# Rows of an expert's later places: gathered in quarter rows by 32 slots, and turned by VectorE in 32x32 squares instead of by TensorE

## The chip, the cores and the metric

The kernel runs on one core of one Trainium2 chip. The metric is the device time of one launch in microseconds (us), lower is better. Before the change three runs took 564.17, 568.13 and 568.21 us, median 568.13. The hardware profile was taken from one more execution, which took 564.15 us by its own clock and whose span, from the first to the last instruction, is 561.9 us.

## The reference, cut to what matters

Two steps, all in float32. A gated linear recurrence over 768 steps for 4 batches of 8 heads with 48 columns gives 3072 rows of 384 values. A mixture of experts without dropping then sends every row to one of 8 experts.

```
for t in range(S):                       # S = 768, per batch and head, state 48 x 48 complex
    S_re, S_im = a[t] * (S_re, S_im) + (k[t] outer v[t], 0)
    y[:, :, t] = q[t] @ S_re
x = y as (3072, 384)
expert = argmax(x @ w_gate); gate = softmax(x @ w_gate)[expert]
for e in range(8):                       # rows of expert e
    out[rows] = gate[rows] * (relu(x[rows] @ w1[e]) @ w2[e])     # w1[e] 384 x 1024, w2[e] 1024 x 384
```

## The kernel before

**Recurrence.** The first 272 us or so are the recurrence in chunks of 128 steps (6 chunks `u`, 4 batches `b`). TensorE does the chunk products, ScalarE and VectorE the gates, the rotations and the evictions. `finish` writes each finished 128 x 384 block of rows to a DRAM buffer `xd`. The order of this stage comes from a table `WHEN` of priorities, written out by hand: `put(t, f)` gives the instructions of `f` the priority `t`, and a scheduler lays each engine's queue out by it. `warm` issues matmuls that only keep TensorE running in the first microseconds.

**Routing.** `route` counts, for a group of chunks, which row goes to which expert, and adds it to `slots`, which holds for each expert and slot (slot = tile of 128 times lane) the row to read, the row to write and the gate. `first_place` names the busiest expert early; `places` orders the rest by their counts. An expert's position in that order is its place. Place `i` has room for `CAPS[i]` rows (448, 416, 416, 408, 400, 384, 376, 360), that is 4 tiles of 128 slots for places 0 to 4 and 3 tiles for 5 to 7; where a count is over its room, a slow path that is compiled in runs, which is not the case for these inputs. `gates_of_places` turns `slots` into `tok` (row to read), `row` (row to write) and `gate`, by place.

**Experts.** From about 272 us the 8 places are worked one after the other. Below, "place i" means the expert of place i, and (i, t) its tile t. Each has these steps:

- `load_w(i)`: SyncE loads w1 as `wa` (partition p, block k holds row 128k + p) and w2 as `wb`. Buffers alternate between two pools, so `wa` of place i + 2 waits until place i has done its first product, and `wb` until it has done its second.
- `gather(i)`: GpSimd (POOL) issues one indirect DMA for each tile of 128 slots: partition p gets the whole row of slot p (1536 bytes) of `xd`. The buffer `xg` alternates too, so the gather of place i + 2 waits until place i has been turned.
- `turn(i)`: the rows have to stand in columns for the product. TensorE transposes each 128 x 128 block with a matmul against `ident` into PSUM (`tp`, line 599), and ScalarE or VectorE copies it to `xt` (line 606). For the next place this is called inside `expert`, by `between`, two tiles before the end.
- `expert(i)`: the first product `hps` runs over 8 blocks `f` of 128 hidden units, all slots of the place at once; blocks alternate between ScalarE (odd f, line 633) and VectorE (even f, line 635) for the relu into `ht`. The second product `yps` runs tile by tile; VectorE multiplies it by the gate into `y` (line 647). A last tile of at most 64 rows is summed from parts: ScalarE copies to `z`, VectorE adds (lines 658 and 660) and multiplies (line 661).
- `scatter`: GpSimd writes the tile's rows to `out` by an indirect DMA (line 611).

The buffers that matter here: `psH` has 4 PSUM banks for `hps`, `psO` 2 for `yps`, `yp` has 3 buffers `y`. So a `y` waits until the scatter three tiles earlier has landed, and block f of `hps` waits until block f - 4 has been evicted. The scatters write one tensor, so each of them also waits until the one before it has landed. All gathers and scatters stand in one queue, POOL's, and run in its order.

`in_range(j)` reads the gates `a_re` and `a_im` once more in 6 parts (tiles `rc`, 768 KB each) and checks their range on VectorE, two passes for each part into `junk` (line 860). It only has to be done before the end.

Of the kernel before, what the change touches and what calls it, by code (L numbers as in the profile page):

```python
# [10 lines left out]
FP = mybir.dt.float32  # L11
I32 = mybir.dt.int32
# [10 lines left out]
LN_CAP = math.log(0.999)  # L23
A_MIN = 0.61
T_MAX = 1.5
CAPS = (448, 416, 416, 408, 400, 384, 376, 360)


# [8 lines left out]
def kernel(  # L37
# [28 lines left out]
    def mm(o, lhsT, rhs, start=True, stop=True):  # L66
        T["mm"] = nc.tensor.matmul(o, lhsT=lhsT, rhs=rhs, start=start, stop=stop, skip_group_check=True)  # L67
        return T["mm"]
# [9 lines left out]
    def const(shape, name, dt=FP):  # L78
        return cp.tile(shape, dt, name=name)
# [40 lines left out]
    for hp in range(HP):  # L120
        nc.gpsimd.tensor_copy(out=back[:, hp, 0:D], in_=ident[:, 0:D])
        nc.gpsimd.tensor_copy(out=back[:, hp, D:DD], in_=ident[:, 64 : 64 + D])

    M = const([P, NU, B, H], "M")
    acc = const([P, E], "acc")
# [263 lines left out]
    def small(shape, name, dt=FP):  # L389
        return ch.tile(shape, dt, tag=name, name=name, bufs=1)  # L390
# [64 lines left out]
    EARLY = 2  # L455
    owner = const([P, E], "owner", I32)
    own0 = const([P, 1], "own0", I32)
    tok = const([P, E, CT], "tok", I32)
    row = const([P, E, CT], "row", I32)
    gate = const([P, E, CT], "gate")  # L460
    over = const([P, 1], "over")
# [43 lines left out]
    def to_read(f, o):  # L505

        ts(out=o, in0=f, scalar1=-1.0, scalar2=0.0, op0=OP.add, op1=OP.max)
# [37 lines left out]
    def gates_of_places():  # L545
        f = small([P, E, CT], "fi")
        by_place(f, 2)
        to_read(f, tok)
        by_place(f, 0)
        to_write(f, row)  # L550
        by_place(gate, 1)
        cmp = small([P, E, E], "cmp")
        tt(out=cmp, in0=T["po"], in1=bc(T["cnt"], 1, E), op=OP.mult)
        o = small([P, E], "t8")
        nc.vector.reduce_sum(o, cmp, axis=AX_X)
        tt(out=o, in0=o, in1=caps, op=OP.is_gt)
        nc.vector.reduce_sum(over, o, axis=AX_X)


    def tiles(i):  # L560
        return -(-CAPS[i] // P)

    def load_w(i, after=None):
        o = own0 if i == 0 else owner[:, i : i + 1]
        ev = nc.sync.value_load(o[0:1, 0:1], min_val=0, max_val=E - 1)
        wa = EP[i % 2].tile([P, KD, F], FP, tag="wa", name="wa")
        ins = nc.sync.dma_start(out=wa, in_=w1[ds(ev, 1)].rearrange("o (i p) f -> p (o i) f", p=P))
        if after is not None:
            tc.add_manual_dep(ins.ins, after.ins.name, SYNC, reason="rows first")
        wb = EP[i % 2].tile([P, KF, DM], FP, tag="wb", name="wb")  # L570
        nc.sync.dma_start(out=wb, in_=w2[ds(ev, 1)].rearrange("o (i p) d -> p (o i) d", p=P))
        T["w", i] = wa, wb

    def gather(i, t0, t1, rows=N):

        if t0 == 0:
            T["xg", i] = EP[i % 2].tile([P, CT, DM], FP, tag="xg", name="xg")
        for t in range(t0, t1):
            n = min(P, CAPS[i] - t * P)
            nc.gpsimd.indirect_dma_start(  # L580
                out=T["xg", i][0:n, t],
                out_offset=None,
                in_=xd[0:rows, :],
                in_offset=bass.IndirectOffsetOnAxis(ap=tok[0:n, i, t : t + 1], axis=0),
                bounds_check=rows - 1,
                oob_is_err=False,
            )

    def turn(i, t0, t1, ps, end=None):

        xg = T["xg", i]
        if t0 == 0:
            T["xt", i] = EP[i % 2].tile([P, KD, CAPS[0]], FP, tag="xt", name="xt")
        c0, c1 = t0 * P, min(CAPS[i], t1 * P)
        for d in range(KD):
            tp = ps.tile([P, 512], FP, tag="tp", name="tp")
            for t in range(t0, t1):
                n = min(P, CAPS[i] - t * P)
                ins = nc.tensor.transpose(  # L599
                    out=tp[:, (t - t0) * P : (t - t0) * P + n],  # L600
                    in_=xg[0:n, t, d * P : (d + 1) * P],
                    identity=ident[0:n, 0:n],
                )
                if end is not None:
                    behind(ins, [end])
            T["turned"] = (nc.scalar.copy if d % 2 else nc.vector.tensor_copy)(
                out=T["xt", i][:, d, c0:c1], in_=tp[:, 0 : c1 - c0]
            )
# [11 lines left out]
    def expert(i, t0, t1, psH, psO, yp, between=None):  # L620

        xt = T["xt", i]
        wa, wb = T["w", i]
        if t0 == 0:
            T["ht", i] = EP[i % 2].tile([P, KF, CAPS[0]], FP, tag="ht", name="ht")
        ht = T["ht", i]
        c0, c1 = t0 * P, min(CAPS[i], t1 * P)
        for f in range(KF):
            ps = psH.tile([P, 512], FP, tag="tp" if psH is psT else "h", name="hps")[:, 0 : c1 - c0]
            for d in range(KD):  # L630
                mm(ps, wa[:, d, f * P : (f + 1) * P], xt[:, d, c0:c1], d == 0, d == KD - 1)
            if f % 2:
                nc.scalar.activation(out=ht[:, f, c0:c1], in_=ps, func=AF.Relu)  # L633
            else:
                ts(out=ht[:, f, c0:c1], in0=ps, scalar1=0.0, scalar2=None, op0=OP.max)  # L635
        for t in range(t0, t1):
            if t == t1 - 2 and between is not None:
                between()
            n = min(P, CAPS[i] - t * P)
            ps = psO.tile([P, DM], FP, tag="at" if psO is psA else "y", padded_shape=[P, 512], name="yps")  # L640
            g = gate[0:n, i, t : t + 1]
            y = yp.tile([P, DM], FP, tag="y", name="y")
            hs = ht[:, :, t * P : t * P + n]
            if n > 64:
                for f in range(KF):
                    mm(ps[0:n], hs[:, f], wb[:, f], f == 0, f == KF - 1)
                ts(out=y[0:n], in0=ps[0:n], scalar1=g, scalar2=None, op0=OP.mult)  # L647
            else:

                w = 32 if n <= 32 else 64  # L650
                parts = P // w
                for f in range(KF):
                    j = f % parts
                    mm(ps[j * w : j * w + n], hs[:, f], wb[:, f], f < parts, f >= KF - parts)
                z = yp.tile([P, DM], FP, tag="z", name="z")
                for j in range(1, parts):
                    nc.scalar.copy(out=z[j * w : j * w + n], in_=ps[j * w : j * w + n])
                tt(out=y[0:n], in0=ps[0:n], in1=z[w : w + n], op=OP.add)
                for j in range(2, parts):
                    tt(out=y[0:n], in0=y[0:n], in1=z[j * w : j * w + n], op=OP.add)  # L660
                ts(out=y[0:n], in0=y[0:n], scalar1=g, scalar2=None, op0=OP.mult)
            scatter(y, n, i, t)

    def early(t0, t1, end):

        turn(0, t0, t1, psT, end)
        expert(0, t0, t1, psT, psA, EP["y"])


    def put(t, f, *a):  # L670
# [5 lines left out]
        "l1": 0, "l2": 1, "p0": 2, "p1": 4, "p2": 4, "p3": 2, "p4": 4, "p5": 3, "s0.0.0": -8.68, "c0": True,  # L676
        "w0": -2.82, "s0.1.0": -7.5, "s0.2.0": -5.29, "s0.0.1": -10.26, "w1": -3, "s0.1.1": -8.3, "s0.2.1": -3.21,
        "s0.0.2": -9.64, "w2": -3, "s0.1.2": -6.91, "s0.0.3": -6.55, "w3": -3, "s0.1.3": -6.6, "h1": True,
        "s1.0.0": -2.81, "c1": False, "s1.1.0": -4.38, "s1.0.1": -4.06, "s1.1.1": -3.59, "d0.0": -3.83, "d0.1": -1.67,
        "TR0": -3, "a0.0": -3.0, "a0.1": -2.9, "a0.2": -2.8, "t0.0": -2.5, "r0.0": -0.4, "p.0": -1.18, "t0.1": -0.55,  # L680
        "r0.1": -1.5, "p.1": -0.32, "t0.2": -1.22, "r0.2": -1.0, "a1": -1.69, "LE1": -1.01, "s0.2.2": -0.84,
        "s0.2.3": -0.8, "d0.2": -0.76, "s1.0.2": -3.39, "s1.1.2": -3.19, "s1.0.3": -2.99, "s1.1.3": -2.79,
        "d1.0": -2.33, "d1.1": -1.18, "h2": False, "s2.0.0": -5.0, "c2": False, "s2.0.1": -6.16, "s2.0.2": -4.19,
        "s2.0.3": -6.99, "TR1": -1.69, "t1.0": -1.85, "r1.0": -1.59, "t1.1": -0.53, "r1.1": 0.42, "a2": -4.5,
        "results0": 1.02, "results1": 1.04, "state": 1.61, "evict": 1.11, "scores0": -0.86, "scores1": 0.42,
        "outer": 0.43, "finish": 1.53, "products": -1.42, "LE2": -6.28, "d2.0": -3, "d2.1": 0.0, "h3": False,
# [1 line left out]
        "r2.0": -3.02, "t2.1": -1.45, "r2.1": 0.68, "a3": -3.28, "LE3": -4.96, "d3.0": -2.87, "d3.1": -1.87,  # L688
        "h4": False, "s4.0.0": -7.27, "c4": False, "s4.0.1": -7.25, "g2": -3.01, "TR3": -2.37, "t3.0": -2.37,
        "r3.0": -1.87, "t3.1": -2.78, "r3.1": -0.87, "a4": -4.45, "LE4": -3.65, "s4.0.2": -7.47, "s4.0.3": -6.41,  # L690
        "d4.0": -2.59, "d4.1": -1.42, "h5": False, "s5.0.0": -6.32, "c5": False, "s5.0.1": -7.01, "s5.0.2": -6.82,
        "s5.0.3": -6.62, "TR4": -1.22, "t4.0": -2.13, "r4.0": -0.31, "t4.1": -0.56, "r4.1": 0.83, "a5": -6.92,
        "LE5": -5.71, "d5.0": -3.39, "d5.1": -1.51, "g4": -2.93, "TR5": -2.92, "t5.0": -2.34, "r5.0": -2,
        "t5.1": -2.31, "r5.1": -1,
    }

# [138 lines left out]
    T["second"]()  # L835
    gates_of_places()
    gather(0, EARLY, tiles(0))
    early(0, EARLY, end)
    att.close()

# [326 lines left out]
```

## Time and profile before

| what | value |
|---|---|
| median of 3 runs | 568.13 us (564.17 to 568.21) |
| profiled execution, own time | 564.15 us |
| its span | 561.9 us |
| TensorE busy, share of the span | 529.7 us, 94% |
| VectorE busy | 286.5 us, 51% |
| ScalarE busy | 217.8 us, 39% |
| GpSimd busy | 68.8 us, 12% (94 instructions) |
| mean granted TensorE clock | 0.99 |
| mean DMA rate | 131 GB/s over the span |

How to read it: TensorE has work in 94% of the span, and from 299 us to the end of the last product at 552 us it has no gap that the profile shows. A share of busy time is an average over the launch. [...] In the views below, PE is TensorE, PEld its weight loads, DVE VectorE, ACT ScalarE, POOL GpSimd and SP SyncE. L599 is line 599 of the kernel before.

### The profile page before, as it was taken

How to read it: one execution, taken by the hardware profiler on the slowest of the kernel's cores; microseconds unless marked ns; L12 is line 12 of the kernel's file. 1: busy time of each engine (PE TensorE's matmuls, PEld its weight loads, DVE VectorE, ACT ScalarE, POOL GpSimd, SP SyncE). 2: the span in 40 equal slices, each digit the busy share in tenths (PEclk: the TensorE clock that was granted, in tenths of full speed). 3: DMA queues.
4: the chain of work that ended last, by engine and by line, in shares of the span. 5: the costliest groups of instructions: out<-in, count | busy, mean ns of one | idle time of the engine just before them, and what ended most of it. 6: DMA issues, size and time to landing. Idle time of an engine off the chain costs nothing.

```text
span 561.9 us, 8229 instructions
## 1 busy us (share of the span) xinstructions
PE 529.7 (94%) x3221; PEld 376.7 (67%) x3221; DVE 286.5 (51%) x584; ACT 217.8 (39%) x330; POOL 68.8 (12%) x94
## 2 busy tenths in 40 slices
PE   3889979999999999999899999999999999999993
PEld 2666858877888888888768555555555555565651
DVE  5478687787889888784565174303113031211110
ACT  6867988786588764553201010101101011010100
POOL 2000000000000000001045301403031040101001
PEclk9979999999999999999999999999999999999998
DMA  9956691847646825404369975534234342230000
GB/s 166 205 80 102 112 148 35 160 76 151 117 86 123 160 58 118 72 30 173 139 255 313 387 281 223 179 127 147 59 144 144 127 153 89 83 121 25 15 14 29
DMA packets 166053, 73.39 MB, mean 131 GB/s; under 512 B 147725, under 2 KB 159031, under 8 KB 166008
## 3 DMA queue, kind: packets, MB, share of 16 engines
q1 hardware_dynamic: 162456, 63.12, 46.4%
q0 software_dynamic: 3552, 9.68, 5.0%
q8 instruction: 27, 0.44, 0.3%
q14 instruction: 18, 0.15, 0.1%
HBM read 63.26 MB, written 9.73 MB: 130 GB/s over the span
## 4 chain that ended last, share of the span: by engine, by line
PE 81%; DVE 6%; ACT 5%; DMA 4%; issue 2%; POOL 0%; ACTq 0%; DVEq 0%
PE yps L67 23%; PE hps L67 23%; PE tp L326 7%; PE at L67 6%; PE yt L67 6%; PE cst L67 4%; PE dk L67 3%; PE xb L67 3%; PE csl L67 2%; PE tp L599 2%; DMA xd<-x 2%; DMA xg<-xd,tok 1%; ACT R L169 1%; PE sp L67 1%; DVE ai L216 1%
## 5 line engine op out<-in xcount | busy, mean ns | idle before, releaser
L67 PE MATMUL yps<-wb,ht 128*128 128x384 f32 (+6 forms) x464 | 136.8, 489 | 0.0
L67 PE MATMUL hps<-xt,wa 128*128 128x416 f32 (+7 forms) x432 | 132.4, 465 | 0.0
L67 PEld LDWEIGHTS hps<-xt,wa 128*128 128x128 f32 x432 | 79.9, 190 | 50.1 <-issue 23.5
L67 PEld LDWEIGHTS yps<-wb,ht 128*128 128x128 f32 (+6 forms) x464 | 74.1, 175 | 52.9 <-issue 8.1
L633 ACT ACTIVATE ht<-hps 128x416 f32<-128x416 f32 (+7 forms) x36 | 16.8, 468 | 139.5 <-PE hps L67 128.3
L647 DVE TENSOR_SCALAR y<-yps,gate 128x384 f32<-128x384 f32 (+2 forms) x24 | 14.8, 617 | 102.6 <-PE yps L67 102.6
L67 PE MATMUL at<-qt,kt 96*128 96x128 f32 x384 | 54.2, 281 | 0.0
L611 POOL DMA_INDIRECT out_dram<-y,row x29 | 29.4, 1014 | 195.2 <-DVE y L647 166.9
L67 PEld LDWEIGHTS at<-qt,kt 96*128 96x128 f32 x384 | 47.6, 191 | 4.2 <-issue 1.5
L635 DVE TENSOR_SCALAR ht<-hps 128x416 f32<-128x416 f32 (+7 forms) x36 | 18.8, 525 | 60.6 <-PE hps L67 60.6
L334 DVE TENSOR_TENSOR am<-at,tri 128x512 f32<-128x512 f32 x48 | 33.0, 688 | 20.8 <-PE at L67 20.5
L67 PE MATMUL yt<-am,v 128*48 128x128 f32 x384 | 43.0, 281 | 0.6 <-DVE am L334 0.6
L580 POOL DMA_INDIRECT xg<-xd,tok x29 | 32.0, 1104 | 77.5 <-PE tp L326 40.3
L67 PE MATMUL yt<-qt,G 96*48 96x128 f32 x320 | 36.7, 274 | 0.0
L326 PE MATMUL tp<-ident,K 128*96 128x128 f32 x192 | 33.0, 283 | 1.8 <-ACT kt L328 0.9
L326 PE MATMUL tp<-ident,Q 128*96 128x128 f32 x192 | 32.9, 277 | 0.0
L328 ACT COPY kt<-tp 96x512 f32<-96x512 f32 x48 | 28.0, 583 | 11.9 <-PE tp L326 11.7
L67 PE MATMUL dk<-v,K 128*96 128x48 f32 x320 | 32.6, 243 | 0.0
L67 PEld LDWEIGHTS dk<-v,K 128*96 128x96 f32 x320 | 31.9, 166 | 0.8 <-issue 0.5
L67 PEld LDWEIGHTS yt<-am,v 128*48 128x48 f32 x384 | 24.8, 122 | 8.2 <-DVE am L334 2.2
L255 POOL DMA_DIRECT2D ai<-cd x4 | 3.4, 842 | 211.9 <-ACT R L169 100.5
L328 ACT COPY qt<-tp 96x512 f32<-96x512 f32 x48 | 28.1, 586 | 2.9 <-PE tp L326 2.9
(155 smaller groups left out, 664.1 us busy)
## 6 DMA issues: line engine op xcount, KB each, us to landing
wa<-in_moe_w_dram SPq DMA_DIRECT2D x8, 1536.0 KB
wb<-in_moe_w_dram SPq DMA_DIRECT2D x8, 1536.0 KB
q<-in_q_dram SPq DMA_DIRECT2D x12, 384.0 KB
k<-in_k_dram SPq DMA_DIRECT2D x12, 384.0 KB
v<-in_v_dram SPq DMA_DIRECT2D x12, 384.0 KB
xd<-x SPq DMA_DIRECT2D x24, 192.0 KB
rc<-in_a_re_dram SPq DMA_DIRECT2D x6, 768.0 KB
rc<-in_a_im_dram SPq DMA_DIRECT2D x6, 768.0 KB
```

Source lines behind the costliest of these rows:

```text
L67: T["mm"] = nc.tensor.matmul(o, lhsT=lhsT, rhs=rhs, start=start, stop=stop, skip_group_check=True)
L169: ins = nc.scalar.activation(**kw)
L216: tt(out=ai, in0=ai, in1=R, op=OP.mult)
L326: nc.tensor.transpose(out=tp[0:DD, j], in_=X[:, hg * 4 + j], identity=ident)
L328: nc.scalar.copy(out=t[0:DD], in_=tp[0:DD])
L334: tt(out=am, in0=at, in1=bc(tri, 1, 4), op=OP.mult)
L580: nc.gpsimd.indirect_dma_start(out=T["xg", i][0:n, t], out_offset=None, in_=xd[0:rows, :], in_offset=bass.IndirectOffsetOnAxis(ap=tok[0:n, ...
L599: ins = nc.tensor.transpose(out=tp[:, (t - t0) * P : (t - t0) * P + n], in_=xg[0:n, t, d * P : (d + 1) * P], identity=ident[0:n, 0:n],)
L611: nc.gpsimd.indirect_dma_start(out=out, out_offset=bass.IndirectOffsetOnAxis(ap=row[0:n, i, t : t + 1], axis=0), in_=y[0:n], in_offset=Non ...
L633: nc.scalar.activation(out=ht[:, f, c0:c1], in_=ps, func=AF.Relu)
L635: ts(out=ht[:, f, c0:c1], in0=ps, scalar1=0.0, scalar2=None, op0=OP.max)
L647: ts(out=y[0:n], in0=ps[0:n], scalar1=g, scalar2=None, op0=OP.mult)
```

## The change

The places 2 to 7 (the third to the eighth) no longer use TensorE to turn their rows. Places 0 and 1 stay as they were (`SQ = 2`).

- The DRAM rows are seen as 12288 quarter rows of 96 values. Each gather fetches, for 32 slots, the four quarters: partition 32a + s gets quarter a of the row of slot s. A place needs one gather for each 32 slots: 13 for places 2 to 4 (13 x 32 = 416), 12 for places 5 to 7, where it had 4 or 3.
- The list of quarter rows, `tok4[32a + s] = 4 * row + a`, is made once by `squares`: four small matmuls spread the row numbers over the four groups of partitions, and one VectorE operation adds the number of the quarter. `tok` itself is kept for places 0 and 1 only.
- One VectorE transpose turns the whole place in squares of 32 x 32, which stay within their 32 partitions. It is held behind the last VectorE relu of the place before (`behind(T["turned"], [T["held"]])`).
- In `xt`, partition 32a + x, block k then stands for column 96a + 32k + x. `load_w` loads w1 in the same order, in four DMAs of 32 partitions for places 2 to 7 where it was one of 128.
- Six values of `WHEN` differ.

```diff
+SQ = 2
+Q4 = 32
+    quarter = const([P, 1], "quarter")
+    for a in range(4):
+        nc.gpsimd.memset(quarter[a * Q4 : (a + 1) * Q4], float(a))
...
-    tok = const([P, E, CT], "tok", I32)
+    tok = const([P, SQ, CT], "tok", I32)
+    tok4 = const([P, E, CT, 4], "tok4", I32)
...
     def gates_of_places():
         f = small([P, E, CT], "fi")
         by_place(f, 2)
-        to_read(f, tok)
+        to_read(f, f)
+        nc.vector.tensor_copy(out=tok, in_=f[:, 0:SQ])
+        T["fi"] = f
+        f = small([P, E, CT], "fj")
         by_place(f, 0)
...
+    def squares():
+        t = ch.tile([P, HB * H, D], FP, tag="Qe", name="square", bufs=1)
+        t = t.rearrange("p h d -> p (h d)")[:, 0 : 4 * P].rearrange("p (b a s) -> p b a s", b=4, a=4)
+        for a in range(4):
+            ts(out=t[:, :, a], in0=ident.rearrange("p (b s) -> p b s", b=4), scalar1=4.0, scalar2=None, op0=OP.mult)
+        sq = psD.tile([P, 4, E * CT], FP, tag="dk", padded_shape=[P, 4, P], name="sq")
+        for b in range(4):
+            mm(sq[:, b], t[:, b].rearrange("p a s -> p (a s)"), T["fi"].rearrange("p e t -> p (e t)"))
+        ts(out=tok4.rearrange("p e t b -> p b (e t)"), in0=sq, scalar1=quarter[:, 0:1], scalar2=None, op0=OP.add)
...
     def load_w(i, after=None):
-        ins = nc.sync.dma_start(out=wa, in_=w1[ds(ev, 1)].rearrange("o (i p) f -> p (o i) f", p=P))
+        parts = [(slice(0, P), w1[ds(ev, 1)].rearrange("o (k p) f -> p (o k) f", p=P))]
+        if i >= SQ:
+            w = w1[ds(ev, 1)].rearrange("o (a k j) f -> a j (o k) f", a=4, k=KD)
+            parts = [(slice(a * Q4, (a + 1) * Q4), w[a]) for a in range(4)]
+        for p, w in parts:
+            ins = nc.sync.dma_start(out=wa[p], in_=w)
...
     def gather(i, t0, t1, rows=N):
-        for t in range(t0, t1):
-            n = min(P, CAPS[i] - t * P)
+        if i < SQ:
+            view, w = xd[0:rows, :], DM
+            parts = [(min(P, c1 - t * P), t, tok[:, i, t : t + 1]) for t in range(t0, t1)]
+        else:
+            view, w = xd.rearrange("n (a c) -> (n a) c", a=4), DM // 4
+            parts = [(P, j, tok4[:, i, j // 4, j % 4 : j % 4 + 1]) for j in range(4 * t0, -(-c1 // Q4))]
+        for n, j, ap in parts:
             nc.gpsimd.indirect_dma_start(
-                out=T["xg", i][0:n, t],
+                out=T["xg", i][0:n, j * w : (j + 1) * w],
...
     def turn(i, t0, t1, ps, end=None):
+        if i >= SQ:
+            j1 = -(-c1 // Q4)
+            T["turned"] = nc.vector.transpose(
+                out=T["xt", i][:, :, c0 : j1 * Q4].rearrange("p k (j s) -> p j k s", s=Q4),
+                in_=xg[:, c0 // Q4 * (DM // 4) : j1 * (DM // 4)].rearrange("p (j k x) -> p j k x", x=Q4, k=KD),
+            )
+            behind(T["turned"], [T["held"]])
+            return
         for d in range(KD):
             tp = ps.tile([P, 512], FP, tag="tp", name="tp")
...
-                ts(out=ht[:, f, c0:c1], in0=ps, scalar1=0.0, scalar2=None, op0=OP.max)
+                T["held"] = ts(out=ht[:, f, c0:c1], in0=ps, scalar1=0.0, scalar2=None, op0=OP.max)
...
     # WHEN
-        "d0.0": -3.83  "r0.1": -1.5   "s2.0.1": -6.16  "d4.0": -2.59  "s5.0.2": -6.82  "TR5": -2.92
+        "d0.0": -3.18  "r0.1": -1.55  "s2.0.1": -6.37  "d4.0": -2.54  "s5.0.2": -6.74  "TR5": -3.13
...
     gather(0, EARLY, tiles(0))
+    squares()
     early(0, EARLY, end)
```

## The prediction

> **What bounds the kernel now.** I read three views in this order. First the page, for the engines and the chain that ended last.
>
> ```profile
> PE 529.7 (94%) x3221; PEld 376.7 (67%) x3221; DVE 286.5 (51%) x584; ACT 217.8 (39%) x330; POOL 68.8 (12%) x94
> PE 81%; DVE 6%; ACT 5%; DMA 4%; issue 2%; POOL 0%; ACTq 0%; DVEq 0%
> ```
>
> TensorE is the bound, and POOL is not on the chain at all. Then the same chain in order of time, from 388 us: places 3 and 4.
>
> ```profile
> 388.06 16.64 PE hps L67 x48
> 404.70 10.32 PE yps L67 x32
> 415.02 1.12 PE tp L599 x8
> 416.14 0.84 PE yps L67 x2
> 416.98 0.49 PE tp L599 x4
> 417.47 6.13 PE yps L67 x30
> 423.61 16.32 PE hps L67 x48
> ```
>
> The pieces touch: nothing waits, so each microsecond of `tp` taken from TensorE moves the end. A place lasts 16.64 + 17.29 us without its transposes (1.61). Last, POOL in order of time, with VectorE's pass over `junk` beside it.
>
> ```profile
> 299.54 1.75 DVE L860 SCALAR_TENSOR_TENSOR junk<-rc,rc 128x1536 f32<-128x1536 f32 x1
> 299.96 2.21 POOL L580 DMA_INDIRECT xg<-xd,tok  x1 [0.31 <-issue]
> ...
> 314.45 1.04 POOL L611 DMA_INDIRECT out_dram<-y,row  x1 [1.12 <-DVE y L647]
> 321.51 0.94 POOL L611 DMA_INDIRECT out_dram<-y,row  x1 [6.01 <-DMA out_dram<-y,row]
> ...
> 382.19 1.05 POOL L580 DMA_INDIRECT xg<-xd,tok  x1 [0.84 <-PE tp L599]
> 383.55 1.01 POOL L580 DMA_INDIRECT xg<-xd,tok  x1 [0.31 <-issue]
> 384.87 1.00 POOL L580 DMA_INDIRECT xg<-xd,tok  x1 [0.30 <-issue]
> 387.57 1.02 POOL L611 DMA_INDIRECT out_dram<-y,row  x1 [1.69 <-DVE y L647]
> 393.11 0.89 POOL L611 DMA_INDIRECT out_dram<-y,row  x1 [4.52 <-DMA out_dram<-y,row]
> ```
>
> Columns: start, length, engine, line. Three prices: a gather occupies POOL for 1.33 us start to start (1.36 and 1.32 here), whether it has 128 rows or 32 (0.91 to 1.05 us long). A scatter may start 5.5 us after the one before it (387.57 to 393.11), 7.1 us where DMA is saturated (314.45 to 321.51). And a gather under a `junk` pass takes 2.21 us instead of 1.02, the median.
>
> [...] 32 rows cost POOL what 128 do, so a quarter of the bytes for a gather will not make it cheaper. [...]
>
> **The change part by part.**
>
> *Removed: transposes on TensorE.* The chain's `tp` pieces for the places turned: 1.67 (at 343.5), 1.64 (379.4), 1.61 (above), 1.17, 1.15, 1.07. Sum 8.31 us, all on the path. The copies beside them (13 on VectorE of 0.56 and 7 on ScalarE, all places) lie beside TensorE and are worth nothing.
>
> *Added: one VectorE transpose for each place.* 39 squares, 1248 elements a lane. Nearest row: `junk`, 1536 elements in 1.76 us, so 1.43 us. [...] It stands behind the last VectorE relu, where VectorE has nothing to do until the first `y`, 5.2 us later, and TensorE needs `xt` only 17 us later. I take it as hidden; it would show above some 5 us.
>
> *Added: `squares`.* Four VectorE operations of about 0.2 us lie in the routing before `first_place`, where VectorE idles 1.38 us before `slots`. The four matmuls (32 columns; `sp`, eight records of 96 columns, lasted 0.87 us) stand on TensorE after six `hps` of the early part, at 283.5, and the row numbers are ready at 283.3. Then `tok` comes some 0.5 us later (two small products ahead of it, then a copy), and with it the gather of place 0's late tiles, for which TensorE waits at 291. The two overlap: 0.6 us, between 0 and 1.5.
>
> *Moved: weights.* Four DMAs of 32 partitions for one. They are issued on SP at 0.4 us each when the buffer is free, some 45 us before use (307 for a first product at 352). Hidden. In SP's queue the loads of `rc` slip behind place 3's `wb`; so eight of twelve `junk` passes move from place 1 into places 2 and 3, two of four directly after the transpose. This frees DMA in 307 to 350 us, loads it after 351, and puts `junk` over gathers.
>
> *Moved: `WHEN`.* Some twenty exchanges in the queues of the recurrence, none of amounts. In 46 to 260 us TensorE is busy 207.8 of 214 us. I take 0, between -2 and +2.
>
> *Added: gathers, and a new wait.* 75 gathers take the place of 21. In the queue of the built kernel, the 12 first gathers of place 4 stand ahead of scatter (1,0), and those of places 5, 6, 7 ahead of the first scatters of places 2, 3, 4; they can start only when the transpose two places earlier is done. The last `y` of such a place (32 rows or less) needs the buffer of its first tile, so it waits for that scatter to land. Behind this `y` on VectorE stands the relu of block 0 of the next place. ScalarE's odd blocks go on, and TensorE stops at block 4, which needs the bank of block 0. Step by step, TensorE 0.6 us later than before:
>
> - Place 2's last eleven and place 3's first twelve gathers start at 305.0: 23 x 1.33 = 30.6, until 335.6. Scatter (0,2) at 335.6, a gather, scatter (0,3) at 341.1 (5.5 later).
> - Place 4: 12 x 1.33 from 342.4 to 358.4. Scatter (1,0) at 358.4; place 3's `wb` and three `rc` have just been issued, so I take 6.5 us (between 5.5 and 7.1): landed at 364.9. Two adds and the relu (1.6): 366.5.
> - TensorE begins place 2 at 316.8 + 16.96 + 17.30 = 351.1 and wants block 4 at 359.6. **Stall 6.9 us.**
> - Scatters (1,1) 364.9, (1,2), (1,3), then place 5's gathers: with 4.5 us each where nothing else moves (an estimate: at 375.2 the data of a scatter had moved 2.4 us after its start) POOL is free at 375.2, the transpose is done at 375. Gathers 16.0 and 1.2 for `junk`: scatter (2,0) at 392.4, landed 398.9, relu done 400.5. Place 2 ends at 375.0 + 17.3 = 392.3, block 4 at 400.6: stall 0; with 5.5 for each scatter 3.5. I take 1.8, the middle.
> - Place 3 in the same way: scatter (3,0) lands at about 434, block 4 of place 4 comes at 436: no stall. Places 5 to 7 have three tiles and no such last tile.
>
> *Sum.* -8.3 + 0.6 + 6.9 + 1.8 = +1.0 us against the profiled execution, 564.15 (span 561.9 and 2.25 around it): 565.2. The median of the runs shown lies 4.0 above that execution, so the forecast for the median is 568.13 + 1.0 = 569.1. A measurement of this kernel can tell about 1% (5.7 us) from no change.
>
> **Rivals.**
>
> *A, the forecast: POOL's queue takes back what TensorE is given.* For it: the prices above, and the order of the queue. Against it: the stall is a difference of two long sums (36 gathers against 43 us), so 0.05 us on each gather is 1.9 us. Own range 565 to 575.
>
> *B, the queue holds.* If gathers of quarter rows went out every 1.15 us, scatter (1,0) would be issued at 358.4 - 36 x 0.18 = 352 and land at 357 with 5 us; no stall: 568.1 - 7.7 = 560.4. For it: block 0's four banks give 8.5 us of cover. Against it: no gather in the trace is shorter than 0.91 us, and the gap of 0.30 is constant.
>
> *C, slower: POOL becomes the bound of places 2 to 5.* Its cycle is four scatters in a row and 12 gathers: 3 x 5.5 + 1.3 + 16.0 + 1.2 = 35.0 us with every scatter at 5.5, TensorE's own is 33.9. Above 33.9 the cover of block 4 is used up at place 3, and each further microsecond is paid at places 3, 4 and 5 and once at place 2. With a gather at 1.45 us: 4.3 us more at place 2 (36 x 0.12) and about 4 more at the three others: 577.5. For it: [...] `rc` now loads beside the scatters. Against it: place 4 onwards has DMA to spare (29% busy after 352).
>
> *D, the transposes are above 5 us or the recurrence's new order costs:* 574. The order counts agree otherwise, and the counts of matmuls are equal.
>
> **How the numbers follow.** A 0.53 (within 1% 0.39, slower 0.12, faster 0.02), B 0.15 (faster 0.12, within 0.03), C 0.27 (slower 0.26, within 0.01), D 0.05 (slower). Faster 0.14, same 0.43, slower 0.43. The likeliest is A, 569.1. The range 562 to 581 leaves out most of B and the far end of C (a gather at 1.5 us).
>
> **What would show it.** Right: no L599 rows after 310 us; a transpose row of about 1.4 us; 75 gathers 1.33 apart; a gap on TensorE of 5 to 9 us in the fifth block of place 2 (about 360 us), released by VectorE's relu of `hps`, which itself follows `y` L702 waiting for DMA; a smaller one or none in place 3. Wrong: no gap at 360 (B), gaps of several us in places 3, 4 and 5 as well, or gathers more than 1.4 apart (C), VectorE waiting in front of the transpose, or a recurrence that ends more than 2 us away from before (D).

## The result, and the profile after

Four runs of the changed kernel took 570.57, 571.55, 575.01 and 577.36 us, median 573.28. The kernel before, on the same occasions, has a median of 566.49. The ratio is 1.0152, 95% interval 1.0112 to 1.0192: slower, by some 6 to 11 us. Ratios here and below leave out executions more than 1.5% above the fastest of the same kernel. The profiled execution is the longest of the four, 577.36 us, with a span of 575.6. It is 13.7 us longer than the profiled span before, where the medians differ by 6.8.

The page and the groups first (the last line is a group: busy time, mean ns, then the idle time before it):

```profile
PE 527.7 (92%) x3166; PEld 373.8 (65%) x3166; DVE 288.1 (50%) x584; ACT 214.9 (37%) x324; POOL 125.2 (22%) x152
PE 21%; issue 2%; POOL 2%; DMA 1%; DVE 0%; POOLq 0%; DVEq 0%
...
L633 DVE STREAM_TRANSPOSE xt<-xg 128x1248 f32<-128x1248 f32 (+1 forms) x6 | 8.5, 1418 | 0.0
```

TensorE is busy 2.0 us less, with 55 instructions gone, in a span that is 13.7 us longer: it stands idle for 47.9 us instead of 32.2. The chain's shares can't be held against those of before, since it was followed back to 411.7 us only, some 26% of the span; POOL's gathers stand on it now (2%). VectorE's six turns take 1.42 us each and have no idle time ahead of them: the part of the change that replaces the transposes works as forecast.

Where the waits are, the timeline of TensorE shows (start, length, line, tile, matmuls; in brackets the idle time before and what ended it):

```profile
315.28 10.74 PE L69 MATMUL hps<-xt,wa 128*128 128x416 f32 x30
329.63 3.76 PE L69 MATMUL hps<-xt,wa 128*128 128x416 f32 x6 [3.61 <-issue]
337.42 7.07 PE L69 MATMUL hps<-xt,wa 128*128 128x416 f32 x12 [4.03 <-issue]
...
344.33 17.07 PE L69 MATMUL yps<-wb,ht 128*128 128x384 f32 x64
361.33 17.03 PE L69 MATMUL hps<-xt,wa 128*128 128x416 f32 x48
...
405.99 8.49 PE L69 MATMUL hps<-xt,wa 128*128 128x408 f32 x24 [2.31 <-DVE ht L679]
...
431.30 8.33 PE L69 MATMUL hps<-xt,wa 128*128 128x400 f32 x24
441.61 10.02 PE L69 MATMUL hps<-xt,wa 128*128 128x400 f32 x24 [1.98 <-DVE ht L679]
```

Before, place 1's first product had no gap:

```profile
316.17 17.03 PE L67 MATMUL hps<-xt,wa 128*128 128x416 f32 x48
```

Three things are to be seen. The first product of place 2 (361.33), where the prediction had its stall of 6.9 us, has no gap. Places 3 and 4 have one each behind their fourth block, of 2.31 and 1.98 us. And place 1, which the change does not touch, takes 29.05 us for its first product (315.28 to 344.33); before it took 16.86 (316.17 to 333.03). Of the 12.2 us, 7.6 are the two gaps; in the other 4.6 TensorE works, but slower: its granted clock was 0.50 from 329.6 to 332 and from 336 to 342 us.

The chain in order of time shows the stall of place 4 link by link:

```profile
432.15 1.00 POOL xg L616
...
433.45 6.37 DMA out_dram<-y,row
...
439.94 0.56 DVE y L702
440.52 0.55 DVE y L704
441.07 0.49 DVE ht L679
441.61 10.02 PE hps L69 x24
```

A scatter stands behind the gathers of a later place, its landing frees a buffer `y`, the short last tile is added up on VectorE, and only then comes the relu that frees a bank for TensorE. That is the mechanism of the forecast, which had it at places 2 and 3. The 24 matmuls behind it take 10.02 us instead of the 8.33 of the first 24, since the granted clock was down to 0.50 from 442 to 445 us, after the gap.

The gaps of place 1 are of another kind. ScalarE and VectorE in the same stretch:

```profile
316.38 0.47 ACT L701 COPY z<-yps 64x384 f32<-64x384 f32 x1 [9.23 <-PE hps L69]
329.06 0.52 ACT L677 ACTIVATE ht<-hps 128x416 f32<-128x416 f32 x1 [12.21 <-remote]
...
322.05 0.59 DVE L679 TENSOR_SCALAR ht<-hps 128x416 f32<-128x416 f32 x1 [4.16 <-PE hps L69]
336.77 0.59 DVE L679 TENSOR_SCALAR ht<-hps 128x416 f32<-128x416 f32 x1 [14.14 <-remote]
```

Before, the relu of block 1 began 4.5 us behind the start of the product (316.17), when two blocks were through; now it begins 13.8 us behind it (315.28):

```profile
320.66 0.52 ACT L633 ACTIVATE ht<-hps 128x416 f32<-128x416 f32 x1 [3.90 <-PE hps L67]
```

In the changed kernel TensorE does a block of six matmuls in 2.1 us (five blocks in 10.74), so the blocks 0, 1 and 2 were through at about 317.6, 319.7 and 321.8. Their relus start at 322.05, 329.06 and 336.77, that is 4, 9 and 15 us late, on two engines that stood idle and whose only wait here is for TensorE. "Remote" is the profile's word for a wait that ended with a signal which it can put down to no instruction. TensorE, in turn, starts 0.05 us after the relu of block 1 ends (329.58 to 329.63): in that direction nothing is late. The profile gives modelled ends for matmuls, so the record alone does not tell a slow matmul from a slow signal. But blocks 3 and 4 stand ahead of block 5 on TensorE, which began at 329.63, and their relus started at 340.33 and 340.40 all the same. That speaks for the signal, though no run shows the signal itself. I call this "late signals" below.

One more cost lies behind the last product. After the last scatter two long instructions stand in POOL's queue (count, then shortest, median and longest ns). Before:

```profile
L892 POOLq INC_SWDGE_SEM  x1: 1447/1447/1447, 554.4 to 554.4; - x1
L1162 POOLq DRAIN  x3: 50/113/5133, 555.9 to 561.6; - x3
```

After:

```profile
L937 POOLq INC_SWDGE_SEM  x1: 2525/2525/2525, 562.7 to 562.7; - x1
L1207 POOLq DRAIN  x3: 50/113/9543, 565.2 to 575.4; - x3
```

That is 1.08 and 4.41 us more, 5.5 together, at the very end, with no engine busy beside them. With 54 DMAs more on POOL (116 instead of 62) it is 0.102 us each.

The 13.7 us then add up: the first product of place 1 begins 0.9 earlier, place 1 loses 12.2, the rest up to the last product gains 3.1 (transposes against the stalls of places 3 and 4), the tail costs 5.5.

### The profile page after: what moved, and what is told of

It reads as the page before. It is cut to its first block, busy times and chain, and to the rows that moved or that the text cites. A ratio compares the mean times of both kernels' runs of the same rounds, so it can differ in the third digit from the quotient of the medians.

```text
span 575.6 us, 8293 instructions
## 1 busy us (share of the span) xinstructions
PE 527.7 (92%) x3166; PEld 373.8 (65%) x3166; DVE 288.1 (50%) x584; ACT 214.9 (37%) x324; POOL 125.2 (22%) x152
## 5 line engine op out<-in xcount | busy, mean ns | idle before, releaser
L69 PE MATMUL hps<-xt,wa 128*128 128x416 f32 (+7 forms) x432 | 139.4, 481 | 11.9 <-issue 7.6
L69 PE MATMUL yps<-wb,ht 128*128 128x384 f32 (+6 forms) x464 | 134.2, 487 | 0.0
L69 PEld LDWEIGHTS hps<-xt,wa 128*128 128x128 f32 x432 | 82.1, 196 | 66.5 <-issue 36.1
L616 POOL DMA_INDIRECT xg<-xd,tok x83 | 86.7, 1045 | 104.8 <-PE tp L332 40.4
L655 POOL DMA_INDIRECT out_dram<-y,row x29 | 30.7, 1060 | 121.2 <-DVE y L691 66.4
L701 ACT COPY z<-yps 32x384 f32<-32x384 f32 (+3 forms) x13 | 6.1, 471 | 84.9 <-remote 56.8
```

The lines of the kernel that those rows point to most:

```text
L616: nc.gpsimd.indirect_dma_start(out=T["xg", i][0:n, j * w : (j + 1) * w], out_offset=None, in_=view, in_offset=bass.IndirectOffsetOnAxis(ap ...
L655: nc.gpsimd.indirect_dma_start(out=out, out_offset=bass.IndirectOffsetOnAxis(ap=row[0:n, i, t : t + 1], axis=0), in_=y[0:n], in_offset=Non ...
```

## The experiments

Each comparison ran on one chip with the kernel before beside it. There were four, on chips that I call A, B, C and D. Before had 565.1, 565.0, 565.3 and 564.8 us on them: the chips are alike for it. From the start of place 1's first product to the start of place 7's second one (the "stretch"), the profile before has 220.26 us, to a hundredth the same in both runs of it with extra gathers of 384 bytes on chip B. So I compare that stretch too: it leaves out the recurrence, behind which place 1's first product begins anywhere between 313.3 and 317.7 us in the profiles of kernels that share it.

### On chip A: gathers or weight loads?

One load of the weights:

```
-        if i >= SQ:
+        if False:
             w = w1[ds(ev, 1)].rearrange("o (a k j) f -> a j (o k) f", a=4, k=KD)
```

> The changed kernel with the weights wa of places 2 to 7 fetched by one DMA of 128 partitions again instead of four of 32 (w1's rows then stand in their old order, so the first product of these places multiplies the wrong rows: that part of the computation is changed). Gathers and turns stay as changed. Theory G (the row of quarter gathers on POOL delays TensorE's signals in the first product of place 1 and holds the scatters back at places 3 and 4): about 12 us of gaps in place 1 stay, and the time stays 5 to 8 us above the kernel before. Theory L (the four loads of 32 partitions, at about half the usual rate, are what delays place 1): the gaps in place 1 are gone, the stalls of 2.3 and 2.0 us at places 3 and 4 may stay, and the time is 3 to 6 us below the kernel before.

Measured: 570.99 us, ratio 1.006 (1.003 to 1.009); by the medians 5.9 us above before. The delays vary from one execution to the next (563.57 to 576.99 us). Profiled at 575.42 us, one of the longer ones:

```profile
329.65 3.92 PE L69 MATMUL hps<-xt,wa 128*128 128x416 f32 x6 [2.88 <-issue]
...
371.44 11.48 PE L69 MATMUL hps<-xt,wa 128*128 128x416 f32 x24 [3.60 <-DVE ht L679]
```

The gaps of place 1 stay (this one, and 1.11 and 1.78 us behind it): the four loads are not their cause, theory L falls (it had 3 to 6 us below before). And here place 2 has its stall behind the fourth block, 3.60 us; VectorE's row ahead of it says why:

```profile
369.76 0.55 DVE L702 TENSOR_TENSOR y<-yps,z 32x384 f32<-32x384 f32 x1 [9.64 <-DMA out_dram<-y,row]
```

Gathers of whole rows, with the rest as changed (`tok` again holds the rows of all places, not shown):

```
-        if i < SQ:
+        if True:
             view, w = xd[0:rows, :], DM
-            parts = [(min(P, c1 - t * P), t, tok[:, i, t : t + 1]) for t in range(t0, t1)]
+            parts = [(min(P, c1 - t * P) if i < SQ else P, t, tok[:, i, t : t + 1]) for t in range(t0, t1)]
```

> The changed kernel with the rows of places 2 to 7 gathered as before, 128 whole rows in one gather, 21 gathers instead of 75 (the squares of 32 then lie in the wrong places of xt: these places compute with misplaced rows). The four loads of 32 partitions and VectorE's turns stay. Theory G: no gap in place 1, no stall at places 3 and 4; 8.3 us of transposes are gone and nothing takes them back: 7 to 9 us below the kernel before, about 558. Theory L: the 12 us in place 1 stay, the stalls of 4.3 us go: 2 to 4 us above the kernel before.

Measured: 555.04 us, ratio 0.9798 (0.9747 to 0.9849), 8.5 to 14.3 us below before. The first product of place 1 in its profile:

```profile
317.66 17.03 PE L69 MATMUL hps<-xt,wa 128*128 128x416 f32 x48
```

No gap anywhere, the stretch is 210.70 us, the tail as before (1447 and 5133 ns again). So the gathers are the cause on this chip (theory G), and 9.56 us is what the removal of the transposes is worth. What in the gathers it is, this run doesn't tell: their number, their rows of 384 bytes and how closely they stand were all changed at once. I had 8.31, the pieces of `tp` alone; the remaining 1.25 lies at places 1 to 3, 0.4 us each, by which a second product that is not cut into three pieces is shorter in the chain (16.90 us against 10.32 + 0.84 + 6.13 = 17.29 at place 3). At places 4 to 6 it is under 0.1 each.

Both edits:

> Both edits: rows of places 2 to 7 gathered by 128 as before, wa in one load as before, and VectorE's turn in squares of 32 kept (rows and weight rows of these places are then misplaced). What is left of the change is the removal of TensorE's transposes, squares() and the recurrence's order. Theories G and L both expect no gap: 8 to 9 us below the kernel before, about 558. If the gaps of place 1 still stand here, neither gathers nor loads make them.

Measured: 555.60 us, ratio 0.9825 (0.9782 to 0.9868), stretch 210.70. No difference from the run above: the four loads of 32 partitions cost nothing, hidden as forecast. They do run slower. While place 2's four are in flight in the changed kernel (310 to 318 us), DMA moves 194 to 210 GB/s at a busy share of 1.03 to 1.04; in the kernel before, with one load of 128 partitions, it moves 375 to 391 in the same stretch (share 1.04 to 1.05). The first run above, with one load and the rest as changed, has 397 GB/s from 301 to 316 us, where the changed kernel has 301 (302 to 317 us). Why they are slower, no run shows.

Places 5 to 7 only:

```
-SQ = 2
+SQ = 5
```

> The changed kernel with SQ = 5: only places 5, 6 and 7 are gathered in quarters and turned by VectorE; places 2, 3 and 4 as before. Nothing of the computation is left out. 1.17 + 1.15 + 1.07 = 3.4 us of transposes go. Theory G with the delay bound to a long row of gathers in a busy stage: place 5's gathers come one place ahead of its use, when DMA has little to do, so no gaps in place 1 and no stall there: 3 to 4 us below the kernel before. If a row of gathers delays TensorE's signals wherever it stands: gaps of several us in place 3 or 4 instead, and 3 to 8 us above the kernel before. Theory L gives 3 to 4 us below only if three loads of 32 partitions hurt less than six.

Measured: 560.43 us, ratio 0.9894 (0.9854 to 0.9935). The stretch is 216.81, 3.45 less than before, and the tail 2.7 us longer (1980 and 7338 ns, 27 DMAs more). That makes -0.7 us. The medians differ by 4.7; the rest must lie before place 1, and I cannot place it. The profile is the more telling part. ScalarE at place 4, beside place 6's row of gathers (418.29 to 433.98 us, with one scatter in it), and below it TensorE:

```profile
436.05 0.50 ACT L677 ACTIVATE ht<-hps 128x400 f32<-128x400 f32 x1 [5.85 <-remote]
...
424.08 16.39 PE L69 MATMUL hps<-xt,wa 128*128 128x400 f32 x48
```

The relu of block 3 comes 3.7 us after the end of its matmuls (432.4). The late signals have moved with the rows: they are now at places 3 and 4, where the gathers of places 5 and 6 stand, and none is in place 1. Beside a row of 12 they are 1 to 4 us late, which four PSUM banks hide: the 48 matmuls have no gap. In the changed kernel place 2's gathers and place 3's stand in one row of 23 (303.55 to 332.24), beside which they are up to 15 us late.

### On chip B: the buffers of y, and rows of gathers alone

Six buffers for y (the pool's small tiles `z` get six as well):

```
-    yp = pool2("yp", 3, reuse_waits="tile")
+    yp = pool2("yp", 6, reuse_waits="tile")
```

> The changed kernel with six buffers for y instead of three, nothing else, nothing of the computation left out. Theory Y (at places 3 and 4 the last y waits for the buffer of a tile whose scatter stands in POOL's queue behind twelve gathers): the stalls of 2.3 us (place 3) and 2.0 us (place 4) are gone, about 4 us below the changed kernel. The delays of TensorE's signals in place 1 (12 us) stay, since they have nothing to do with these buffers, and so does the tail after the last scatter (13 us). Rival: the delay of the signals is what holds places 3 and 4 too; then the stalls stay.

Measured: 559.05 us, ratio 0.9869 (0.9824 to 0.9915). The stalls are gone, but so is the gap of place 1, which no theory of mine had:

```profile
316.99 17.03 PE L69 MATMUL hps<-xt,wa 128*128 128x416 f32 x48
```

The stretch is 210.70, the same as without the extra gathers. The tail stays (2524 and 9543 ns).

Rows of gathers alone, added to the kernel before (the other two differ in the width, 384 for 96, and in the partitions, 32 for 128):

```
+    def extra():
+        view = xd.rearrange("n (a c) -> (n a) c", c=96)
+        per = RW // 96
+        for j in range(24):
+            nc.gpsimd.indirect_dma_start(
+                out=extra_rows[0:128, j % per * 96 : (j % per + 1) * 96],
+                out_offset=None,
+                in_=view,
+                in_offset=bass.IndirectOffsetOnAxis(ap=tok[0:128, 7, 0:1], axis=0),
...
+        if i == 6:
+            extra()
```

> The kernel before with 24 gathers more, back to back on POOL ahead of place 6 (128 rows of 384 bytes each, into a buffer that nobody reads). Theory N (a row of POOL's DMAs, whatever they hold, delays TensorE's signals): the relus of place 6 come late from about the sixth gather on, by several us near the row's end. [...] Theory 0 (a quiet stage of DMA has no delay): none. For the tail: 24 gathers x 0.102 us = 2.4 us more between the last scatter and the end (two points so far: 7.8 us with 62 POOL DMAs, 13.3 us with 116).

> As the run with 24 gathers of 384-byte rows, but with rows of 1536 bytes (four times the bytes[...]). [...] If bytes count: larger. Tail again 2.4 us longer than before.

> As the run with 24 gathers of 384-byte rows, but 32 rows in each gather[...], POOL busy as long. Theory N: the same delays. [...] Tail: 2.4 us if it counts gathers[...].

The scheduler put the row elsewhere: nothing held it back to place 6, and it begins between 291 and 295 us, among the gathers of places 0 to 2. Measured: 567.13 us, 1.0037 (1.0017 to 1.0057), with 384-byte rows; 574.69, 1.0157 (1.0099 to 1.0214), with 1536; 567.84, 1.0038 (1.001 to 1.0067), with 32 rows a gather. On the signals they say nothing more than the run before them: with rows of 8 and more gathers between single scatters from 295 to 343 us, no relu is late on this chip while its engine stands idle for TensorE. On the tail they are clear:

```profile
L910 POOLq INC_SWDGE_SEM  x1: 1927/1927/1927, 554.0 to 554.0; - x1
L1180 POOLq DRAIN  x3: 50/112/7093, 556.0 to 563.6; - x3
```

This is the run with 32 rows; the other two have the same two numbers. So 24 DMAs cost 0.48 + 1.96 = 2.44 us at the end, whatever their rows and bytes: 0.102 us for each DMA, on the same line as 62, 89 and 116 DMAs. The 1.0037 and 1.0038 are 2.1 us, and the stretch is 220.26: the tail is all that such a row costs there. With 1536 bytes the stretch is 5.70 us longer as well, mostly at place 1: the `rc` loads landed later (a `junk` pass began at 339.35 us, after a wait of 7.09 for its `rc`; with 384 bytes at 331.23), the relu of block 6 stood behind two such passes until 342.84, and TensorE waited 2.79 us for it. A scatter waited behind the row too, and the last `y` of place 1 waited 5.48 us for its landing, as in the stalls of places 3 and 4; TensorE lost 0.43 us by it.

### On chip C: the buffers, or the chip?

Both kernels once more, unedited and with six buffers, beside each other.

> The changed kernel once more, unedited, beside the next run on one chip. The run with six buffers for y showed no delayed signals in place 1 (0.04 us), the changed kernel 4 to 14 us, although both have the same instructions on TensorE and POOL up to there. Theory B (the buffers made the difference): the delays are here and not in the next run: some 10 us or more between the two, time 6 to 8 us above the kernel before. Theory C (the delays belong to a chip or to an execution, given many gathers, and have nothing to do with the buffers): both runs show them, or neither does. If neither: this one is 4 us above the next run (the stalls of places 3 and 4) and 1 to 3 us below the kernel before.

> The changed kernel with six buffers for y once more, beside the run of the unedited one on the same chip. Theory B: no delays, 5 to 6 us below the kernel before, as the first time. Theory C: as the run beside it, less the 4 us of stalls at places 3 and 4.

Measured: unedited 574.24 us, 1.0149 (1.0106 to 1.0193); with six buffers 568.94, 1.0071 (1.0043 to 1.0099). Unedited:

```profile
317.64 12.84 PE L69 MATMUL hps<-xt,wa 128*128 128x416 f32 x36
332.85 3.19 PE L69 MATMUL hps<-xt,wa 128*128 128x416 f32 x6 [2.38 <-issue]
...
407.80 7.46 PE L69 MATMUL hps<-xt,wa 128*128 128x408 f32 x21 [3.86 <-DVE ht L679]
```

With six buffers:

```profile
338.19 15.46 PE L69 MATMUL yps<-wb,ht 128*128 128x384 f32 x54 [3.93 <-issue]
...
362.56 8.65 PE L69 MATMUL hps<-xt,wa 128*128 128x416 f32 x24 [0.34 <-DVE ht L679]
```

Both have the late signals, theory C. The buffers do what they were meant to: 5.3 us less by the medians (4 expected), and the 3.86 us at place 3 are gone. With six buffers relus of places 3 and 4 are late too, beside rows of 12 (at place 4 by 2.3 and 3.9 us), again without a gap. The same kernel with six buffers takes 559.05 us on chip B and 568.94 on chip C: the late signals are worth about 10 us there, and B does not have them. They vary on C as they did on A: eight executions took 563.7 to 572.48 us, and the profiled one is the shortest, with 7.1 us more in its stretch than on B.

### On chip D: gathers spread out

Both runs have six buffers for `y`. In the first, `one` issues a gather of the next place and lets it wait for `after`; `todo` lists those of the place:

```
+    def some(n, after):
+        for one, p in T["todo"][:n]:
+            one(*p, after)
+        T["todo"] = T["todo"][n:]
...
             if f % 2:
-                nc.scalar.activation(out=ht[:, f, c0:c1], in_=ps, func=AF.Relu)
+                done = nc.scalar.activation(out=ht[:, f, c0:c1], in_=ps, func=AF.Relu)
             else:
-                T["held"] = ts(out=ht[:, f, c0:c1], in0=ps, scalar1=0.0, scalar2=None, op0=OP.max)
+                done = T["held"] = ts(out=ht[:, f, c0:c1], in0=ps, scalar1=0.0, scalar2=None, op0=OP.max)
+            some(1, done)
```

> The changed kernel with six buffers for y and its quarter gathers spread out: each of the twelve waits for one relu of the place before (2.1 us apart), the rest for its first y's, so that no row of gathers stands in POOL's queue and no scatter stands behind one. Nothing of the computation is left out. Theory R (rows of gathers back to back delay TensorE's signals, on chips that show it at all): relus 0.04 us behind their matmuls everywhere, no gap on TensorE, and about 559 us on any chip (8.3 us of transposes and 0.9 less, 5.5 of tail more: 2 to 5 below the kernel before). Rival M (the number of gathers in the stage decides, not how close they stand): the same delays as in the run beside it. Rival W (pacing makes a gather late): VectorE's turn waits for gathers, and the first product of a place starts late.

> The changed kernel with six buffers for y, gathers in rows as changed: the run that the paced one is held against, on the same chip. If this chip delays signals (two of three so far): delays of 2 to 12 us in place 1 and about 565 to 570 us. If not: none, and about 559, and then the paced run tells only whether pacing costs something.

Measured: 559.30 us, 0.9905 (0.9877 to 0.9932), spread out; 559.06, 0.9901 (0.9864 to 0.9937), in rows. Chip D shows no late signals either, with rows or without, so theory R and rival M are both untried, and whether spreading helps on A and C stays open. What it costs is seen: the stretch is 211.31 instead of 210.70, with one turn a little late, the rival W on a small scale:

```profile
381.98 16.71 PE L69 MATMUL hps<-xt,wa 128*128 128x408 f32 x48 [0.21 <-DVE xt L648]
```

With six buffers the change makes the kernel 1% faster than before on B and D, but 0.7% slower on C. On B and D, -9.56 for the transposes and +5.5 for the tail make -4.1 of the -5.9 and -5.8 us between the medians. With squares at places 5 to 7 alone the kernel was 1.1% faster on A, a chip with late signals; which of the two is the better version was not run on one chip.

## Why the prediction was right or wrong

The time lay in the range (562 to 581). The forecast, 569.1, was 4.2 us low. As a difference it was further off: +1.0 us forecast, +6.8 measured by the medians, since the kernel before had a median 1.6 us lower than the 568.13 from which the forecast started. Term by term errors of both signs met. Forecast were -8.3 (transposes), +0.6 (ahead of place 1), +6.9 (place 2) and +1.8 (place 3). In the profile they are -9.56, -0.9, 0 and +6.5 (places 3 and 4, with the halved clock), and +12.2 and +5.5 come from two costs that the sum did not have: +13.7 in all. That the time came near the forecast is luck in part.

- **Removed transposes, -8.3.** Right in kind and hidden by nothing; mis-sized, 9.56 measured. The sum took the `tp` pieces and missed that cutting the second product costs 0.4 us at each of the places 1 to 3.
- **VectorE's transposes, 0.** Right: 1.47 us (1248 elements) and 1.37 us (1152), forecast 1.43.
- **`squares` and `WHEN`, +0.6 and 0.** Not told apart: place 1 begins 0.9 us earlier, and executions differ by 4 us in that. By the medians, what stretch and tail leave open ahead of place 1 is from 0 (both edits, chip A) to 1.8 us (six buffers, B and D) and 4.0 (`SQ = 5`) in favour of the change; no run has the new `WHEN` alone.
- **Weights, 0.** Right: one load instead of four changes nothing (0.9825 against 0.9798), although DMA moves about half as much beside the four (194 to 210 GB/s against 375 to 391).
- **Prices on POOL.** A gather 1.30 us start to start (1.33 used). An unhindered scatter 3.4 (333.54 to 336.96; I estimated 4.5), a hindered one 7.0 (398.02 to 405.02).
- **Stall at place 2, +6.9.** The step on POOL was right: scatter (1,0) went out at 359.87 us, forecast 358.4. What failed is the time at which TensorE wants the block: place 1 was 12 us late, so the landing was in cover. In the run with one load (chip A) the stall is there, 3.60 us: TensorE comes to place 2 only 2.1 us earlier, but scatter (1,0) goes out 7.2 us later (367.05), behind gathers, one of which holds the chain for 2.44 us (354.29). How large it is on a chip without late signals, with three buffers, was not run. An estimate from the runs with six buffers in rows, on B and D: (1,0) landed at 366.3 and 362.0 us, TensorE wanted block 4 at 359.5 and 356.0, and from the landing to TensorE's restart it takes 1.7 (369.76 to 371.44 with one load), so three buffers would have cost some 8 us. By this the largest term of the forecast was nearly right, and was hidden by a cost that the forecast did not have.
- **Stalls at places 3 and 4, +1.8 and 0.** 2.31 and 1.98, and 1.7 more by the halved clock behind the second; 3.86 at place 3 on chip C. The mechanism is shown by the chain and by its cure (six buffers). The 3.5 us of which 1.8 is half does not come out of the prediction's own steps: two scatters at 5.5 instead of 4.5 move the relu by 2.0, to 402.5 against 400.6, a stall of 1.9.
- **Missing: the tail, +5.5.** The prediction set the sum against the last product and took what lies behind it as fixed. The two instructions stand in the trace of before (1447 and 5133 ns), with POOL's 62 DMAs as their measure, but one trace could not show the slope.
- **Missing: late signals, +12.2 in the profile, about 10 by the medians with six buffers (C against B).** With three buffers part of it stands in the place of the stall at place 2, some 8 us by the estimate above. The prediction gave POOL's queue, DMA and the `junk` passes as what gathers run into. That relus can come late beside a row of them (up to 15 us) shows nowhere in the trace of before, whose rows are of four.

Of the rivals, C (577.5) is 4.2 us away, as far as the forecast, and wrong in what it said: gathers are 1.30 us apart and not 1.45, and POOL is not the bound of places 2 to 5; of its signs, gaps in places 3, 4 and 5, those in 3 and 4 came true (2.31 and 1.98 us). B fails on the gathers, 1.30 and not 1.15 apart; its sign, no gap at 360 us, came true for another reason, the late place 1. D fails on the transposes. That the range held is owed in part to C's width and not to its reason.

What stays open: what beside a row of gathers makes the relus late; why two chips of four show it (which chip gave the first result is not known); and whether the length of a row, the number of gathers or their 384-byte rows decide, for which chip A has only rows of 12 against one of 23. The runs that were to tell them apart stood on chips without late signals.

## What to carry to other kernels

Count what a new DMA on POOL costs at the end of the kernel as well as in its queue: here 0.102 us for each, so 54 small gathers took back more than half of what they made possible. Ask of every gather that is put ahead of a scatter which buffer the scatter frees and who stands behind it in order; more buffers were the cheap cure. And look into a stage that the change does not touch: its gaps, with the halved clock, were the largest single cost, and the idle engines beside it, waiting for a signal that the profile could not place, were the only sign of what made it.

## What the runs showed of the hardware

- POOL's two long instructions at the end grow by 0.020 us (INC_SWDGE_SEM) and 0.082 us (DRAIN) for each DMA that POOL issued: 1447, 1927, 1980 and 2525 ns, and 5133, 7093, 7338 and 9543 ns, for 62, 86, 89 and 116 DMAs. The run with 32 rows of 384 bytes and those with 128 rows of 384 and 1536 bytes have the same two numbers.
- Beside long rows of POOL gathers of 384-byte rows, relus on VectorE and ScalarE began up to 15 us after the end that the profile gives their matmuls, on some chips (A and C here) and not on others (B and D), while TensorE still started 0.05 us after the relu it waited for and POOL kept its 1.30 us for a gather. Rows of 12 gave 1 to 4 us on chip A, a row of 23 up to 15 in the first profile; rows of four, in the kernel with whole-row gathers on chip A, gave none.
- Around some gaps of TensorE its granted clock was halved for some microseconds (0.50 from 329.6 to 332, from 336 to 342 and from 442 to 445 us in the first profile), so these stalls were paid for a second time. Not around all: behind the gaps of 2.31 us (first profile) and 3.86 us (chip C) at place 3 it was 1.00.
- A gather of 16 rows took POOL 1.22 us start to start (356.03 to 357.25 in the kernel before), one of 128 rows 1.30, with 1536 bytes in a row (309.76 to 311.06, kernel before) or 384 (308.80 to 310.10, first profile), where no `junk` pass stands beside it. Beside one it was busy for 2.30 us instead of 1.00 (380.63, first profile).
